# A second product half in float32r: three passes for the even blocks, two banks a block, and a ring of token columns

## The chip, the cores and the metric

The kernel runs on one core of a Trainium2 chip. The time is device microseconds of that core, from start to end of one execution. Five engines take part, each with a queue of its own that it works through in order: PE (matrix products; its weight loads are shown as PEld), ACT, DVE and POOL (operations on tiles, element by element), and SP, which here only issues DMA transfers. SBUF is the memory on the chip, with 128 partitions; PSUM is the memory that PE writes its products to, in eight banks of 128 x 512 float32. An engine waits for another through semaphores.

## What is computed

Two stages. The first is an attention with a polynomial feature map, for 4 batches x 4 heads x 1088 tokens of 32 numbers:

```
phi(x)[i, j] = (S1 @ x)[i] * (S2 @ x)[j]          # 8 x 8 = 64 features
kv = sum over tokens of phi(k) v;  z = sum over tokens of phi(k)
attn = (phi(q) @ kv) / (phi(q) @ z + 1e-6)
```

Its result, with the four heads side by side, is x: 4352 tokens of 128 numbers. The second stage is a mixture of four experts, weighted by p, the normalised domain_probs:

```
out = sum over e of  p[:, e] * (relu(x @ w1[e]) @ w2[e])      # w1[e]: 128 x 1024, w2[e]: 1024 x 128
```

All inputs and the output are float32.

## The kernel before

**Chunks, steps and products.** The 4352 tokens are columns: x is held transposed in one SBUF tile `xT`, 128 x 4352. They are cut into eleven chunks (line 69) of 128, 448, six of 512, 320, 256 and 128 columns. A chunk takes 16 steps: 4 experts x 4 steps, and each step makes two blocks (j = 0, 1) of 128 hidden units. The first and the last chunk are "plain": PE multiplies in float32. In the nine chunks between, 144 steps in all, the first product (lines 829 to 841) goes in three passes of the faster format float32r: the weights are split into `wa`, `wb`, `wd` (`weight_parts`, line 675) and the token columns into `xa`, `xb`, `xd` (`token_parts`, line 687), so that wa·xa + wb·xb into one bank `g1` (lines 833 and 834), scaled, less wd·xd in a second bank `g2` (line 835), gives the float32 product. ACT copies `g1` to SBUF with the scale (L837), DVE subtracts `g2` (L839), and ACT applies the rectifier (L848), which is put behind the next block's copy.

**Second product.** `second` (line 850) runs two steps behind `first` (`LA = 2`). For each block PE multiplies the hidden block with `w2_sb` in float32 (L885), which the profile shows as two matmuls a block. All eight blocks of one expert, four steps, add up in one bank `o`. Then `gather` (line 909) copies the bank to `ev` on ACT (L913), multiplies it with the expert's gate on POOL (L917 or L919) and adds it to `total` (L920). After the fourth expert `turn_back` transposes `total` (L897) and stores it. In the main loop (lines 952 to 995) `gather` is only appended to the chain `ending`; its copy is issued one step later, after that step's `first` and `second`.

**PSUM.** The eight banks: two for `h` (g1), two for `g` (g2), one for `o`, one for `f` and two, `den` and `num`, for the attention.

**Order.** Nothing reorders instructions: the order in which the program issues them is each engine's queue. The attention is written as a generator of small pieces (`front`, line 760; a unit of query columns has 20 pieces, a batch's keys 19), and `work()`, called after each block of a step, issues as many pieces as the remaining attention needs to be done in time (`rate`, line 959; a reserve of eight pieces). About half of the pieces hold a DVE operation, a few a group of PE matmuls through the helper of line 204. Results of the attention go to a DRAM tile `xd` and back into `xT` through SP's queue (lines 611 to 623). `token_parts` for the next chunk is issued in the last step of a chunk (line 972), gates are loaded at the steps of line 982, and `weight_parts` is issued one piece a step from step 7 on (line 970).

Of the kernel before, what the change touches and what calls it, by code (L numbers as in the profile page):

```python
# [24 lines left out]
def kernel(  # L25
# [52 lines left out]
    ps_h = ctx.enter_context(tc.tile_pool(name="ps_h", bufs=2, space=bass.MemoryType.PSUM))  # L78
    ps_g = ctx.enter_context(tc.tile_pool(name="ps_g", bufs=2, space=bass.MemoryType.PSUM))
# [48 lines left out]
    w1_sb = cpool.tile([P, E, F], F32, name="w1_sb")  # L128
    w2_sb = cpool.tile([P, E, FB, DM], F32, name="w2_sb")

    def load_w1(e):
        nc.sync.dma_start(w1_sb[:, e, :], w1[e])

    def load_w2(e):
        nc.sync.dma_start(w2_sb[:, e], w2[e].rearrange("(f p) d -> p f d", p=P))
# [25 lines left out]
    load_w2(0)  # L161
    for e in range(1, E):
        load_w1(e)
        load_w2(e)
    sk = cpool.tile([P, P], F32, name="sk")
    sp = cpool.tile([32, 3, 2, 32], F32, name="sp")
# [147 lines left out]
    def load_gates(m, experts):  # L314
        for e in experts:
            gate[m, e] = mpool.tile([P, CW], F32, tag="gate", bufs=6, name="gate")
            for b, c, n, at in parts(m):
                nc.sync.dma_start(gate[m, e][:, at : at + n], gates[b, e, c : c + n].partition_broadcast(P))

    xT = cpool.tile([P, B * S], F32, name="xT")  # L320
# [46 lines left out]
    def key_project_wide(b, gi, kf):  # L367

        t0, n = FG[gi]
        if gi == 0:  # L370
            fss[b] = apool.tile([P, 2, NT, 32], F32, tag="fs", name="fs")
            kps[b] = apool.tile([P, NT, 2, P], F32, tag="kp", name="kp")
        for t in range(n):
            for _ in range(2):
                on_side(
                    lambda s: kf[half[s], P * t : P * t + P],
                    lambda s: kT[:, P * (t0 + t) + HP * s : P * (t0 + t) + HP * s + HP],
                    lambda s: sk[:, :],
                    start=True,
                    stop=True,  # L380
                )
        nc.scalar.copy(
            _ap(fss[b], 0, P, 32 * t0, [[32 * NT, 2], [32, n], [1, 32]]), _ap(kf, 0, P, 0, [[32, 2], [P, n], [1, 32]])
        )
# [126 lines left out]
    def attend_first(b, c, n, qp):  # L511

        nd = [psum(ps_n, "den"), psum(ps_n, "num")]
        for _ in range(2):
            on_side(
                lambda s: nd[0][half[s], 0:n],
                lambda s: _ap(vx, 0, P, D, [[0, HP]]),
                lambda s: _ap(eps, 0, P, 0, [[0, n]]),
                start=True,
                stop=False,  # L520
            )
        for i in range(2):
            for _ in range(2):
                on_side(
                    lambda s: nd[i][half[s], 0:n],
                    lambda s: kvzs[b][:, s, 1 - i, :],
                    lambda s: qp[s][:, 0:n],
                    start=(i > 0),
                    stop=True,
                )  # L530
        yield

        rc = apool.tile([P, 2, HP], F32, tag="rd", name="rd")
        for i in range(2):
            by_g = [[32, 4], [1, 16]]
            nc.vector.reciprocal(_ap(rc, 0, P, HP * i, [[16, 4], [1, 16]]), _ap(nd[0], 0, P, 16 * i, by_g))
            nc.vector.tensor_tensor(
                out=_ap(xT, 0, P, HP * i, [[1, 4], [4, 16]]),
                in0=_ap(nd[1], 0, P, 16 * i, by_g),
                in1=_ap(rc, 0, P, HP * i, [[16, 4], [1, 16]]),  # L540
                op=ALU.mult,
            )
        have[0] += n
        yield

    def attend(b, c, n, qp):
# [46 lines left out]
        for c0, T, t0 in laid:  # L593
# [4 lines left out]
            if b == 0 and c == P:  # L598
                for x in range(2):
                    yield  # L600
                    for a in (x, x + 2):
                        run = 32 * T[a // 2]
                        for h in range(H):
                            copy = nc.scalar.copy if h % 2 else nc.gpsimd.tensor_copy
                            at = S * b + c + a // 2 * 64 * T[0] + a % 2 * run
                            copy(xT[32 * h : 32 * h + 32, at : at + run], _ap(y, 32 * a, 32, 32 * T[0] * h, [[1, run]]))
                continue
            m = 64 * sum(T)
            base = xd.offset + P * (S * b + c + c0)
            for a in range(4):  # L610
# [9 lines left out]
            nc.sync.dma_start(  # L620
                xT[:, S * b + c + c0 : S * b + c + c0 + m],
                bass.AP(xd.tensor, base, [[m, P], [1, m]]),
            )
# [5 lines left out]
    def queries(b, c, n):  # L629
        qc = early.pop((b, c), None)  # L630
        if qc is None:
            qT = query_turn(b, c, n)
            yield
            yield
            yield
            qc = psum(ps_f, "f")
            both(qc[:, 0:n], sq[:, :], qT[:, 0:n], start=True, stop=True)
            yield
# [28 lines left out]
    NEAR = 1.0 - 2.0 ** -13  # L667
    wa = cpool.tile([P, E, F], F32R, name="wa")
# [6 lines left out]
    def weight_parts(e):  # L675

        HF = F // 2
        for c in (slice(0, HF), slice(HF, F)):
            nc.scalar.activation(wa[:, e, c], w1_sb[:, e, c], ACTF.Copy, scale=4096.0 * NEAR)
            stt(wb[:, e, c], w1_sb[:, e, c], 4096.0, wa[:, e, c].bitcast(F32), ALU.subtract)  # L680
            yield
            stt(wd[:, e, c], wa[:, e, c].bitcast(F32), R12, wb[:, e, c].bitcast(F32), ALU.subtract)
            yield

    xparts = {}

    def token_parts(m):
# [3 lines left out]
        x = xT[:, START[m] : START[m] + n]  # L691
        nc.scalar.activation(xa[:, 0:n], x, ACTF.Copy, scale=R12 * NEAR)  # L692
        stt(xb[:, 0:n], xa[:, 0:n].bitcast(F32), -4096.0, x, ALU.add)
        nc.vector.tensor_tensor(  # L694
# [4 lines left out]
    def start():  # L699
# [9 lines left out]
        for gi in range(3):  # L709
            kf.append(psum(ps_h, "h") if gi < 2 else psum(ps_g, "g"))  # L710
# [7 lines left out]
        fq = [psum(ps_o, "o"), psum(ps_g, "g"), psum(ps_n, "num")]  # L718
# [34 lines left out]
        early[b, n] = psum(ps_g, "g")  # L753
# [28 lines left out]
    def half_columns(i, hp, c):  # L782

        e, f = divmod(i, NP)
        for j in range(2):
            both(
                hp[:, P * j + c : P * j + c + HP],
                w1_sb[:, e, P * (2 * f + j) : P * (2 * f + j + 1)],
                xT[:, c : c + HP],
                start=True,  # L790
                stop=True,
            )

    def first(i, work):

        m, kq = steps[i]
        n, (e, f) = CHUNKS[m], divmod(kq, NP)
        hd = mpool.tile([P, 2 * CW], F32, tag="hid", bufs=3, name="hid")  # L800
        hid[i] = hd

        if plain(m):
            rectify()
# [5 lines left out]
            else:  # L810
                hp = psum(ps_h, "h")
                for j in range(2):
                    both(
                        hp[:, n * j : n * j + n],
                        w1_sb[:, e, P * (2 * f + j) : P * (2 * f + j + 1)],
                        xT[:, START[m] : START[m] + n],
# [12 lines left out]
        xa, xb, xd_ = (x[:, 0:n] for x in xparts[m])  # L829
        for j in range(2):  # L830
            c = slice(P * (2 * f + j), P * (2 * f + j + 1))
            g1, g2 = psum(ps_h, "h"), psum(ps_g, "g")
# [3 lines left out]
            out = hd[:, n * j : n * j + n]  # L836
            nc.scalar.activation(out, g1[:, 0:n], ACTF.Copy, scale=1.0 + R12)  # L837
            rectify()
            nc.vector.tensor_tensor(out=out, in0=out, in1=g2[:, 0:n], op=ALU.subtract)  # L839
            to_rectify.append(out)  # L840
            work()

    to_rectify = []

    def rectify():
        while to_rectify:
            out = to_rectify.pop(0)
            nc.scalar.activation(out, out, ACTF.Relu)  # L848

    def second(i):  # L850
# [3 lines left out]
        if plain(m):  # L854

            if f == 0:
                acc[m] = psum(ps_g, "g") if e % 2 else psum(ps_o, "o")
            for j in range(2):
                for _ in range(2):
                    on_side(  # L860
                        lambda s: acc[m][half[s], 0:DM],
                        lambda s: hd[:, n * j + HP * s : n * j + HP * s + HP],
                        lambda s: w2_sb[:, e, 2 * f + j, :],
# [3 lines left out]
            if f == NP - 1:  # L867
                p_e = ends[:, 1 if m else 0, e : e + 1]
                if e == 0:
                    total[m] = mpool.tile([P, P], F32, tag="end", name="end")  # L870
# [11 lines left out]
        if f == 0:  # L882
            acc[m, e] = psum(ps_o, "o")
        for j in range(2):
            nc.tensor.matmul(  # L885
                acc[m, e][:, 0:n],
                w2_sb[:, e, 2 * f + j, :],
                hd[:, n * j : n * j + n],
                start=(f == j == 0),
                stop=(f == NP - 1 and j == 1),  # L890
            )
# [17 lines left out]
    def gather(m, e):  # L909
# [3 lines left out]
        nc.scalar.copy(ev[:, 0:n], acc.pop((m, e))[:, 0:n])  # L913
        g = gate.pop((m, e))[:, 0:n]
        if e == 0:
            total[m] = mpool.tile([P, CW], F32, tag="total", name="total")
# [4 lines left out]
        yield  # L921
        if e == E - 1:
# [24 lines left out]
    for i in range(3):  # L947
        begun_hp[i] = psum(ps_h, "h") if i < 2 else psum(ps_g, "g")
        half_columns(i, begun_hp[i], 0)
    to_part = chain.from_iterable(weight_parts(e) for e in range(E))  # L950
    ending = iter(())
    for i in range(len(steps) + LA):
        if i < len(steps):
# [5 lines left out]
            rate = CHUNKS[m] / NQ * max([0] + [(needed[c] + (8 if c > 1 else 4) - done[0]) / (START[c] - gone) for c in range(m + 1, NC)])  # L959
# [10 lines left out]
            if i > NQ - 10:  # L970
                next(to_part, None)
            if kq == NQ - 1 and m + 2 < NC:
# [9 lines left out]
            if m and m + 2 < NC and kq in (LA + 3, NQ - 4):  # L982
                load_gates(m + 1, range(2) if kq == LA + 3 else range(2, E))
# [5 lines left out]
        if i >= LA:  # L989
            second(i - LA)  # L990
            mm, kk = steps[i - LA]
            if kk % NP == NP - 1 and not plain(mm):
                ending = chain(ending, gather(mm, kk // NP))
# [31 lines left out]
```

## Time and profile before

| | us |
|---|---|
| median of three runs (581.96 to 583.17) | 582.67 |
| the profiled execution | 583.37 |
| its span, first to last instruction | 581.6 |
| first plain chunk, attention's start and weights | 0 to 31.4 |
| nine chunks in float32r, 144 steps | 31.4 to 559.1 |
| rest, last plain chunk | 559.1 to 581.6 |
| PE busy in the span | 507.9 |
| ACT, DVE, POOL busy | 328.0, 308.6, 85.4 |

A group in the profile is a line of the kernel, its engine and operation, the tiles it writes and reads, how often it ran, its busy time, the mean duration of one, and the idle time of the engine before it with what ended it. The list of waits sums such idle times: who waited for whom, total, times, longest. A timeline row is start, duration, engine, line, operation, tiles and form; the bracket holds the idle time before it. A matmul's row begins when PE may start it and its end is modelled; the distance between the starts of neighbouring rows tells how long PE was held by one.

### The profile page before, as it was taken

To read this page: it belongs to the slowest core of one execution; us is meant where nothing else is said; L and a number is where in the kernel's file an instruction comes from. 1 tells how busy PE (TensorE), PEld (TensorE's weight loads), DVE (VectorE), ACT (ScalarE), POOL (GpSimd) and SP (SyncE) were. 2 spreads that over 40 slices of the span, in tenths; PEclk is the share of its full clock that TensorE was granted. 3 is DMA by queue.
4 is the path that set the end of the run, shared out by engine and by line. 5 is a ranking of instruction groups with operands and counts; after the bars stand their busy time and mean duration, and the time that the engine had idled before them with its cause. 6 is when DMAs were issued, how large, how long until landed. Compare 5 with 4: busy or idle time off the path is not lost.

```text
span 581.6 us, 8014 instructions
## 1 busy us (share of the span) xinstructions
PE 507.9 (87%) x2823; PEld 320.4 (55%) x2823; DVE 308.6 (53%) x649; ACT 328.0 (56%) x693; POOL 85.4 (15%) x109
## 2 busy tenths in 40 slices
PE   9888888988888979989798898888989988897887
PEld 6855555554454544655454454545445554676777
DVE  6978544564745445375655355246473454444433
ACT  3665565555564664565556565355565565565651
POOL 5200110111110101101110101101101011212110
PEclk9998999999998999999999898889999999999999
DMA  8672140002002042010204011010200200020000
GB/s 226 192 157 64 40 150 19 20 16 73 0 12 67 0 116 72 19 19 17 52 0 92 1 46 18 19 17 2 61 15 11 53 11 10 15 60 0 13 1 16
DMA packets 42576, 26.04 MB, mean 45 GB/s; under 512 B 25928, under 2 KB 38568, under 8 KB 42536
## 3 DMA queue, kind: packets, MB, share of 16 engines
q1 hardware_dynamic: 42520, 25.53, 17.4%
q8 instruction: 22, 0.36, 0.3%
q14 instruction: 18, 0.15, 0.1%
q10 hardware_dynamic: 16, 0.00, 0.0%
HBM read 21.28 MB, written 4.24 MB: 44 GB/s over the span
## 4 chain that ended last, share of the span: by engine, by line
PE 73%; ACT 15%; DVE 8%; issue 2%; DMA 1%; POOL 0%; ACTq 0%; SPq 0%; DVEq 0%
PE o L885 39%; PE h L833 9%; PE h L834 9%; PE g L835 8%; ACT hid L837 6%; ACT hid L848 5%; PE f L204 3%; ACT ev L913 3%; PE den L204 2%; PE h L204 2%; DVE hid L839 1%; DVE qp L504 1%; DVE xd L694 1%; DVE xb L673 1%; PE g L204 1%
## 5 line engine op out<-in xcount | busy, mean ns | idle before, releaser
L839 DVE TENSOR_TENSOR hid<-hid,g 128x512 f32<-128x512 f32 (+3 forms) x288 | 180.3, 626 | 248.1 <-PE h L834 121.4
L885 PE MATMUL o<-hid,w_sb 128*128 128x512 f32 (+3 forms) x576 | 258.0, 572 | 56.3 <-ACT ev L913 56.3
L837 ACT ACTIVATE hid<-h 128x512 f32<-128x512 f32 (+3 forms) x288 | 157.5, 547 | 219.6 <-PE h L834 218.1
L885 PEld LDWEIGHTS o<-hid,w_sb 128*128 128x128 f32 x576 | 105.9, 193 | 136.2 <-ACT ev L913 68.9
L848 ACT ACTIVATE hid<-hid 128x512 f32<-128x512 f32 (+3 forms) x288 | 166.5, 578 | 1.2 <-DVE hid L839 1.2
L833 PE MATMUL h<-xa,wa 128*128 128x512 f32 (+3 forms) x288 | 160.5, 557 | 2.8 <-ACT xa L692 2.4
L834 PE MATMUL h<-xb,wb 128*128 128x512 f32 (+3 forms) x288 | 107.7, 374 | 4.8 <-DVE xb L673 4.7
L835 PE MATMUL g<-xd,wd 128*128 128x512 f32 (+3 forms) x288 | 108.3, 376 | 2.9 <-DVE xd L694 1.6
L919 POOL TENSOR_TENSOR ev<-ev,gate 128x512 f32<-128x512 f32 (+3 forms) x27 | 31.5, 1165 | 342.4 <-ACT ev L913 342.4
L833 PEld LDWEIGHTS h<-xa,wa 128*128 128x128 f32 x288 | 55.7, 193 | 44.5 <-issue 22.4
L834 PEld LDWEIGHTS h<-xb,wb 128*128 128x128 f32 x288 | 55.3, 192 | 38.8 <-issue 26.1
L835 PEld LDWEIGHTS g<-xd,wd 128*128 128x128 f32 x288 | 54.5, 189 | 15.6 <-DVE xd L694 4.3
L920 POOL TENSOR_TENSOR total<-total,ev 128x512 f32<-128x512 f32 (+3 forms) x27 | 31.4, 1164 | 2.1
L917 POOL TENSOR_TENSOR total<-ev,gate 128x512 f32<-128x512 f32 (+3 forms) x9 | 10.8, 1196 | 119.4 <-ACT ev L913 107.0
L504 DVE TENSOR_TENSOR qp<-qa,qb 64x512 f32<-64x512 f32 (+5 forms) x44 | 25.3, 574 | 1.0
L204 PE MATMUL h<-xT,w_sb 128*64 128x128 f32 (+1 forms) x256 | 18.5, 268 | 1.9 <-ACT hid L825 1.9
L825 ACT ACTIVATE hid<-h 128x256 f32<-128x256 f32 x22 | 8.2, 383 | 20.7 <-PE h L204 20.6
L913 ACT COPY ev<-o 128x512 f32<-128x512 f32 (+3 forms) x36 | 19.2, 534 | 0.0
L204 PEld LDWEIGHTS h<-xT,w_sb 128*64 128x64 f32 x256 | 14.1, 137 | 3.8 <-ACT hid L825 2.1
L650 DVE STREAM_SHUFFLE qa<-qf 128x512 f32<-128x512 f32 (+5 forms) x22 | 12.9, 586 | 0.0
L394 DVE TENSOR_TENSOR kp<-fs 128x256 f32<-128x256 f32 (+1 forms) x24 | 10.8, 452 | 0.1
L204 PEld LDWEIGHTS den<-kvx,qp 128*64 128x64 f32 x240 | 8.4, 137 | 3.6 <-PE h L834 2.1
(142 smaller groups left out, 251.2 us busy)
## 6 DMA issues: line engine op xcount, KB each, us to landing
w_sb<-in_moe_w_dram SPq DMA_DIRECT2D x8, 512.0 KB
gate<-gates SPq DMA_DIRECT2D x16, 256.0 KB
kn<-in_k_dram SPq DMA_DIRECT2D x4, 544.0 KB
vn<-in_v_dram SPq DMA_DIRECT2D x16, 128.0 KB
gate<-gates SPq DMA_DIRECT2D x8, 224.0 KB
qn<-in_q_dram SPq DMA_DIRECT2D x2, 544.0 KB
out_dram<-ob SPq DMA_DIRECT2D x16, 64.0 KB
qn<-in_q_dram SPq DMA_DIRECT2D x2, 480.0 KB
```

What stands on the lines that cost most here:

```text
L204: nc.tensor.matmul(out(s), weights(s), moving(s), **flags)
L504: nc.vector.tensor_tensor(out=qp[p][64 * x : 64 * x + 64, 0:n], in0=qa[64 * p : 64 * p + 64, 0:n], in1=qb[64 * p : 64 * p + 64, 0:n], op=A ...
L833: nc.tensor.matmul(g1[:, 0:n], wa[:, e, c], xa, start=True, stop=False)
L834: nc.tensor.matmul(g1[:, 0:n], wb[:, e, c], xb, start=False, stop=True)
L835: nc.tensor.matmul(g2[:, 0:n], wd[:, e, c], xd_, start=True, stop=True)
L837: nc.scalar.activation(out, g1[:, 0:n], ACTF.Copy, scale=1.0 + R12)
L839: nc.vector.tensor_tensor(out=out, in0=out, in1=g2[:, 0:n], op=ALU.subtract)
L848: nc.scalar.activation(out, out, ACTF.Relu)
L885: nc.tensor.matmul(acc[m, e][:, 0:n], w2_sb[:, e, 2 * f + j, :], hd[:, n * j : n * j + n], start=(f == j == 0), stop=(f == NP - 1 and j == 1),
L913: nc.scalar.copy(ev[:, 0:n], acc.pop((m, e))[:, 0:n])
L919: nc.gpsimd.tensor_tensor(out=ev[:, 0:n], in0=ev[:, 0:n], in1=g, op=ALU.mult)
L920: nc.gpsimd.tensor_tensor(out=total[m][:, 0:n], in0=total[m][:, 0:n], in1=ev[:, 0:n], op=ALU.add)
```

## The change

The second product of the even block (j = 0) of each step also goes in three float32r passes. `FK = 1` says that it is the even ones alone.

- The weights: `second_weight_parts` makes `va`, `vb`, `vd` from the even half of w2[e] (one ACT and two DVE operations an expert). They take the memory of w1[e] and w2[e]'s even half, so `load_last` fetches those again for the last chunk, in the middle of the chunk before it.
- The hidden block: instead of one rectifier, ACT makes `hb` and `ha` (`high_parts`), DVE forms `hb` from t and `hb` (`low_parts`, both operands in SBUF) and POOL subtracts them to `hc`. The odd block keeps its rectifier. A tile `t` with two buffers stands between; its buffer is free when both have read it.
- Banks: the expert's sum needs two, `o0` and `o1`. `h` now has three banks for g1 and g2 together; `g` is gone.
- `gather` copies both banks on ACT (`ev`, `ew`) and adds them on POOL ahead of the gate. Its first part is issued at once, in the step that ends the block. The gate of the same expert for the next chunk is loaded one step later; the gates have four buffers in place of six.
- `token_parts` is issued three steps earlier (step 12 of 16, but for the first chunk), and its last operation moves from DVE to POOL. The pace of the pieces aims four steps earlier.
- `xT` is replaced by a ring of three chunks and two small tiles for the plain chunks.
- The weight pieces start two steps earlier. `key_project_wide` and a query product issue one full matmul where two half-column calls stood.

```
     def token_parts(m):
...
-        x = xT[:, START[m] : START[m] + n]
+        ((x, _, _),) = placed(START[m], n)
...
-        nc.vector.tensor_tensor(
+        nc.gpsimd.tensor_tensor(
             out=xd_[:, 0:n], in0=xa[:, 0:n].bitcast(F32), in1=xb[:, 0:n].bitcast(F32), op=ALU.subtract
         )
...
         for j in range(2):
             c = slice(P * (2 * f + j), P * (2 * f + j + 1))
-            g1, g2 = psum(ps_h, "h"), psum(ps_g, "g")
+            g1, g2 = psum(ps_h, "h"), psum(ps_h, "h")
...
-            out = hd[:, n * j : n * j + n]
-            nc.scalar.activation(out, g1[:, 0:n], ACTF.Copy, scale=1.0 + R12)
-            rectify()
-            nc.vector.tensor_tensor(out=out, in0=out, in1=g2[:, 0:n], op=ALU.subtract)
-            to_rectify.append(out)
+            t = mpool.tile([P, CW], F32, tag="t", name="t")[:, 0:n]
+            nc.scalar.activation(t, g1[:, 0:n], ACTF.Copy, scale=1.0 + R12)
+            flush(ACT)
+            nc.vector.tensor_tensor(out=t, in0=t, in1=g2[:, 0:n], op=ALU.subtract)
+            flush()
+            if j < FK:
+                ha, hb, hc = (mpool.tile([P, CW], F32R, tag=f"h{i}", bufs=3, name=f"h{i}")[:, 0:n] for i in "abd")
+                hid[i].append((ha, hb, hc))
+                later[ACT].append(lambda t=t, ha=ha, hb=hb: high_parts(t, ha, hb))
+                later[DVE].append(lambda t=t, ha=ha, hb=hb, hc=hc: low_parts(t, ha, hb, hc))
+            else:
+                u = hidden()[:, 0:n]
+                hid[i].append(u)
+                later[ACT].append(lambda t=t, u=u: nc.scalar.activation(u, t, ACTF.Relu))
             work()
...
+    def high_parts(t, ha, hb):
+        nc.scalar.activation(hb, t, ACTF.Relu, scale=NEAR)
+        nc.scalar.activation(ha, t, ACTF.Relu, scale=NEAR * R12)
+
+    def low_parts(t, ha, hb, hc):
+        nc.vector.scalar_tensor_tensor(
+            out=hb, in0=t, scalar=0.0, in1=hb.bitcast(F32), op0=ALU.max, op1=ALU.subtract
+        )
+        nc.gpsimd.tensor_tensor(out=hc, in0=ha.bitcast(F32), in1=hb.bitcast(F32), op=ALU.subtract)
...
-            acc[m, e] = psum(ps_o, "o")
+            acc[m, e] = psum(ps_o, "o0"), psum(ps_o, "o1")
+        o0, o1 = (o[:, 0:n] for o in acc[m, e])
+        last = f == NP - 1
         for j in range(2):
...
+            if j < FK:
+                (va, vb, vd), (ha, hb, hc) = w2_parts[e], hd[j]
+                nc.tensor.matmul(o0, va[:, f, :], ha, start=(f == j == 0), stop=False)
+                nc.tensor.matmul(o0, vb[:, f, :], hb, start=False, stop=(last and j == FK - 1))
+                nc.tensor.matmul(o1, vd[:, f, :], hc, start=(f == j == 0), stop=False)
+            else:
+                nc.tensor.matmul(o1, w2_of[e, j][:, f, :], hd[j], start=False, stop=(last and j == 1))
...
     def gather(m, e):
...
-        nc.scalar.copy(ev[:, 0:n], acc.pop((m, e))[:, 0:n])
+        ew = mpool.tile([P, CW], F32, tag="ew", bufs=1, name="ew")
+        o0, o1 = acc.pop((m, e))
+        nc.scalar.activation(ev[:, 0:n], o0[:, 0:n], ACTF.Copy, scale=1.0 + R12)
+        nc.scalar.copy(ew[:, 0:n], o1[:, 0:n])
+        nc.gpsimd.tensor_tensor(out=ev[:, 0:n], in0=ev[:, 0:n], in1=ew[:, 0:n], op=ALU.add)
...
         yield
+        if not plain(m + 1):
+            load_gates(m + 1, [e])
...
-            if i > NQ - 10:
+            if i > NQ - 12:
                 next(to_part, None)
-            if kq == NQ - 1 and m + 2 < NC:
+            if kq == NQ - (4 if m else 1) and m + 2 < NC:
...
+            if m == NC - 2 and kq == NQ // 2:
+                while have[0] < B * S:
+                    piece()
+                load_last()
...
             if kk % NP == NP - 1 and not plain(mm):
-                ending = chain(ending, gather(mm, kk // NP))
+                ended = gather(mm, kk // NP)
+                next(ended)
+                ending = chain(ending, ended)
```

## The prediction

> **What bounds the kernel now.** I read the table of engines first, then PE's waits, then the timeline of two ordinary steps and one that opens an expert's block, then the starts of all 144 steps. The profiled execution took 583.37 us for a span of 581.6 us; the sum below is made against 583.37, which is 0.7 us above the median of the runs, 582.67.
>
> ```profile
> PE 507.9 (87%) x2823; PEld 320.4 (55%) x2823; DVE 308.6 (53%) x649; ACT 328.0 (56%) x693; POOL 85.4 (15%) x109
> ...
> L885 PE MATMUL o<-hid,w_sb 128*128 128x512 f32 (+3 forms) x576 | 258.0, 572 | 56.3 <-ACT ev L913 56.3
> ```
> ```profile
> PE o L885 <- ACT ev L913: 56.3, 35, 3.0
> PE h L834 <- DVE xb L673: 4.7, 8, 0.8
> PE h L833 <- ACT xa L692: 2.4, 5, 1.4
> ```
> PE is the bound; no other engine is busy 60% of the span. What PE waits for is almost only the copy of the finished block out of its single bank. The timeline shows the two kinds of step (start, duration, engine, line):
>
> ```profile
> 145.90 0.19 PEld L833 LDWEIGHTS h<-xa,wa 128*128 128x128 f32 x1 [0.24 <-issue]
> ...
> 146.33 0.19 PEld L834 LDWEIGHTS h<-xb,wb 128*128 128x128 f32 x1 [0.24 <-issue]
> ...
> 146.56 0.39 PE L834 MATMUL h<-xb,wb 128*128 128x512 f32 x1
> ...
> 147.05 0.60 ACT L837 ACTIVATE hid<-h 128x512 f32<-128x512 f32 x1 [0.99 <-PE h L834]
> ...
> 147.55 0.62 ACT L848 ACTIVATE hid<-hid 128x512 f32<-128x512 f32 x1
> 147.68 0.69 DVE L839 TENSOR_TENSOR hid<-hid,g 128x512 f32<-128x512 f32 x1 [0.97 <-PE h L834]
> ...
> 149.06 0.59 ACT L913 COPY ev<-o 128x512 f32<-128x512 f32 x1
> ...
> 149.70 0.30 PEld L885 LDWEIGHTS o<-hid,w_sb 128*128 128x128 f32 x2 [2.26 <-ACT ev L913]
> ...
> 151.09 0.19 PEld L833 LDWEIGHTS h<-xa,wa 128*128 128x128 f32 x1 [0.24 <-issue]
> ```
> Steps begin with a weight load of L833. An ordinary step of 512 columns is 3.11 us: its float32r matmuls start 0.23 us apart (six, 1.38), and each of the four halves of the two float32 ones takes 0.43 (1.72). The step above runs from 145.90 to 151.09, 5.19 us, because ACT reaches the copy at 149.06, behind both halves of the next step. So a block's end costs 2.08 us. Over all steps the ordinary ones are 2.72, 3.11, 1.96 and 1.575 us for 448, 512, 320 and 256 columns: 16 x (2.72 + 6 x 3.11 + 1.96 + 1.575) = 398.6 us of the 527.7 us between 31.4 and 559.1. The 36 ends of blocks add 24 x 2.08 + 4 x 1.93 + 4 x 1.62 + 4 x 1.5 = 70 us, chunk starts (waits for xa, xb, xd) about 15, half-clock stretches about 12 (granted clock 0.979 of 581.6 us), attention's matmuls the rest. PE explains the whole middle.
>
> **The terms.** Call a step's first-product matmuls a0 b0 d0 and a1 b1 d1.
>
> 1. *Passes.* One float32 block (2 x 0.43) becomes three float32r (3 x 0.23): -0.17 us a step at 512, and by the same two lengths -0.14, -0.08, -0.04 at 448, 320, 256. 96 x 0.17 + 16 x 0.26 = **-20.5**.
>
> 2. *Three banks where there were four.* Four tiles a step now rotate through three banks, so d1 takes the bank that a0 and b0 filled and waits until ACT has copied it. In the step above b0 streams from 146.56 to 146.79 and the copy starts at 147.05, so 0.72 us after a0's stream begins (146.33); it takes 0.595; PE goes on 0.05 later (ev's end at 149.65, the load at 149.70) and a restart costs 0.11 more (a restarted first half is 0.53 long, not 0.43). d1 ends its stream at 0.72 + 0.595 + 0.05 + 0.11 + 0.23 = 1.705 where it ended at 1.38: +0.325 us. For 448, 320, 256 columns, with their copies of 0.541, 0.434, 0.381: +0.35, +0.40, +0.43. 96 x 0.325 + 16 x 1.18 = +50; some 22 of attention's groups of matmuls (half of some 45) lie between d0 and a1 and cover it: -7. **+43**. So a 512 step goes to 3.11 - 0.17 + 0.325 = 3.26 us: the passes alone lose.
>
> 3. *Block ends.* The copies go into ACT's queue before the next step, onto banks that the next block needs 1.7 us later: -70. What comes instead: two copies (0.5 us apart) hold back the next step's first copy by 0.24 us, and with it d1. Then POOL runs hc, add, multiply, add back to back (4 x 1.28). DVE's new operation (it forms hb from two SBUF operands) can't run beside a POOL operation:
>
> ```profile
> 149.73 1.27 POOL L919 TENSOR_TENSOR ev<-ev,gate 128x512 f32<-128x512 f32 x1 [12.76 <-ACT ev L913]
> 149.95 1.39 DVE L504 TENSOR_TENSOR qp<-qa,qb 64x320 f32<-64x320 f32 x1
> ```
> That L504 form takes 0.48 to 0.49 us in the rows around it; here it ends 0.34 after POOL does. In the other order POOL is stretched (L917 at 118.56: 1.69 us). Laid out by queue, the next step's hb operation is ready about 0.2 us after the multiply has begun and starts 1.07 later; 0.3 of that is slack, 0.75 reaches the following step's first copy, whose buffer t it must free. A chance phase costs less. Between 0.24 and 1.0 us a block; I take 0.9 at 512, in proportion below: **-70 + 29**.
>
> 4. *Tokens.* Chunk starts lose their 15 us; xa, xb (two SBUF operands) and xd, now on POOL at 1.28, cost the steps they fall into about 0.9 each: **-7**. The new tokens need their DMAs four steps earlier; the pace aims at that point with eight pieces to spare, some 3.5 steps, so I cost it at nothing. A late DMA would stop ACT, and PE behind it. SP's gate loads now wait for POOL's multiply, about one step, inside the same reserve.
>
> 5. *DVE and ACT.* ACT gets five operations a step at 0.5 us apart (147.05, 147.55), 2.5, and 0.25 for copies: below 3.26, so no bound. DVE gets three at 0.61 to 0.69 beside attention's 0.8 a step (128 us busy from 200 to 450; the two L839 of the 61 steps in there are 82, so 46 over 61 steps): 2.8 of 3.26. The loop from one step's first copy through subtract, a piece of attention w, subtract and hb to the next first copy is 2.57 + w us, free up to w = 0.69. Single pieces (0.4 to 0.73) fit; a double, about one in six calls, costs up to 0.6, and a product or hb caught by POOL about 0.4. No row shows the queues this full: between 0 and +45; I take **+18**, near the low end, as most pieces fit by their rows.
>
> 6. *Second weights* (4 x one ACT and two DVE operations, 0.63 and 0.69) in the stretch to 60 us, where DVE is busy 16 of every 20 us: 0 to +12, **+7**. The reload of 3.1 MB for the last chunk begins some 15 us before it; at the 169 GB/s of the first 55 us all of it takes 18.6, and the last expert is wanted some 10 us into the chunk. **+1**.
>
> 7. *Clock.* Each half-clock stretch follows a long stop of PE, and most of those stops go: of the 12 us about 3 stay, **-9**. The profile shows no stretch after short stops. The Trainium skill ("TensorE: Matmul & The Clock Gate", section "A second HAM failure mode: psum-queue depth-cycling") speaks against this change: it tells of a kernel whose short idles, from cycling through banks, made the clock fall and recover again and again. That is what term 2 makes; if each of 36 blocks met one stretch of 3.4 us at half speed, my estimate from it would be about +49 us in place of -9. No row here shows it.
>
> Removed half-column calls for keys and queries (0.27 us matmuls two at a time) against full ones: nothing either way, between -2 and +2.
>
> **Sum:** -20.5 + 43 - 41 - 7 + 18 + 7 + 1 - 9 = -8.5: 575 us in the profiled execution, **574** beside the median.
>
> **Rivals.**
> *A, the new waits are mostly covered.* Attention's matmuls and a drifting phase hide them: block ends cost 0.24 (8 us, not 29), term 5 costs 6 and term 2 33. All of it gives 574 - 21 - 12 - 10 = 531, half of it 552: I put **541**. For it: PE was the only full engine. Against: d1's wait is built into every step.
>
> *B, slower: the SBUF read that DVE and POOL share becomes the cycle.* POOL goes from 85 to about 300 us busy (hc 96 x 1.28, 16 x 1.13, 0.87, 0.73, and a third operation a block). If hb or a product waits half a POOL operation (0.64) in every step that carries a piece of attention (w = 0.55), the loop is 2.57 + 0.55 + 0.64 = 3.76, not 3.26: +0.5 in some 75 steps, 38 us, of which 12 are in term 5: **600**. It decides from w + wait above 0.69 us; whether hc falls beside attention's products is set by phase, and I can't exclude it.
>
> *C, a long wait stays.* hc comes late at block ends, or the two copies wait on each other, and half the 70 us remain: 574 + 35 - 15 (the collisions that then fall into the wait) = **594**.
>
> *D, it doesn't do what it says:* the three passes aren't faster than two halves. The six rows of 0.23 speak against that; 574 + 20 = **594**.
>
> **Chances.** Forecast (560 to 581) 0.40; A 0.20; B 0.28; C 0.08; D 0.04. Forecast and A make 0.60 faster and the others 0.40 slower; of these 0.04 and 0.01 lie within 0.2% of 582.67, about what a measurement of this kernel can tell from no change: faster 0.56, same 0.05, slower 0.39. Range: most of A and most of B, **545 to 606**.
>
> **What would show it.** Right: PE's wait on the block's copy gone from its list, a wait of d1 on the first ACT copy in nearly every step (some 0.2 us), ordinary 512 steps of 3.2 to 3.3 us, hb operations longer than 0.69 only beside POOL. Wrong: ordinary steps near 2.94 (term 2), 3.7 and more (B), or half-clock stretches well above seven (term 7).

## The result, and the profile after

The changed kernel takes 575.71 us (median of four runs, 574.72 to 576.13), the kernel before beside it 582.32: a ratio of 0.988, 95% interval 0.986 to 0.990. The prediction said 574. The profiled execution's span went from 581.6 to 572.9 us. Read by stage, from the starts of the 144 steps in both timelines:

| us | before | after | difference |
|---|---|---|---|
| up to the first float32r step | 31.4 | 32.7 | +1.3 |
| chunk of 448 columns | 58.4 | 70.9 | +12.5 |
| six chunks of 512 | 396.2 | 372.8 | -23.4 |
| chunk of 320 | 42.4 | 42.1 | -0.3 |
| chunk of 256 and the rest | 53.2 | 54.4 | +1.2 |

So the six chunks of 512 became 6% faster, and the 448 chunk, which makes the new weights, gave half of that back. The page's table of engines and the top groups of the changed kernel:

```profile
PE 501.9 (88%) x2893; PEld 337.0 (59%) x2893; DVE 432.4 (75%) x792; ACT 424.5 (74%) x877; POOL 318.6 (56%) x298
...
L901 POOL TENSOR_TENSOR hd<-ha,hb 128x512 fp32r<-128x512 f32 (+3 forms) x144 | 173.2, 1203 | 206.5 <-PE h L872 74.9
...
L875 ACT ACTIVATE t<-h 128x512 f32<-128x512 f32 (+3 forms) x288 | 158.9, 552 | 100.9 <-DVE hb L898 47.3
...
L898 DVE SCALAR_TENSOR_TENSOR hb<-t,hb 128x512 fp32r<-128x512 f32 (+3 forms) x144 | 113.8, 790 | 0.3 <-ACT hb L894 0.3
```

and what PE waits for in it (total, times, longest):

```profile
PE h L873 <- ACT t L875: 45.3, 83, 1.6
PE h L871 <- DVE t L877: 11.2, 15, 1.6
PE o L952 <- DVE vd L685: 2.5, 1, 2.5
```

PE is busy for hardly less time than before, three other engines have filled up, and the wait on the block's copy (56.3 us) is gone from the list. In its place stands d1 (second call of L873), which waits for the step's first copy (L875). The timeline of an ordinary step shows it:

```profile
303.60 0.19 PEld L871 LDWEIGHTS h<-xa,wa 128*128 128x128 f32 x1 [0.24 <-issue]
...
303.87 0.68 DVE L898 SCALAR_TENSOR_TENSOR hb<-t,hb 128x512 fp32r<-128x512 f32 x1
...
304.74 0.60 ACT L875 ACTIVATE t<-h 128x512 f32<-128x512 f32 x1 [0.47 <-PE h L872]
...
305.39 0.19 PEld L873 LDWEIGHTS h<-xd,wd 128*128 128x128 f32 x1 [0.48 <-ACT t L875]
...
306.86 0.19 PEld L871 LDWEIGHTS h<-xa,wa 128*128 128x128 f32 x1 [0.24 <-issue]
```

303.60 to 306.86 is 3.26 us; the copy ends at 305.34 and d1's load starts at 305.39. And this is the second step after a block's end, 4.16 us long:

```profile
299.44 0.19 PEld L871 LDWEIGHTS h<-xa,wa 128*128 128x128 f32 x1 [0.24 <-issue]
...
299.54 1.28 POOL L986 TENSOR_TENSOR ev<-ev,gate 128x512 f32<-128x512 f32 x1
299.72 1.66 DVE L898 SCALAR_TENSOR_TENSOR hb<-t,hb 128x512 fp32r<-128x512 f32 x1
...
301.49 0.60 ACT L875 ACTIVATE t<-h 128x512 f32<-128x512 f32 x1 [1.38 <-DVE hb L898]
...
302.14 0.19 PEld L873 LDWEIGHTS h<-xd,wd 128*128 128x128 f32 x1 [1.38 <-ACT t L875]
```

hb is issued 0.18 us after the gate's multiply has begun on POOL, stands until that ends, frees t at 301.38, and only then can the first copy write t and d1 go on. 35 of the 144 hb operations are stretched by over 0.15 us, by 24 us together. Each of the 35 overlaps a POOL operation: 32 began beside the additions and the multiply of a block's end, 3 beside hc. The Trainium skill ("SBUF — State Buffer", section "Who interferes with whom") says that a DVE operation with two SBUF inputs contends with a POOL operation that reads SBUF, that the shared ports are an exclusive lock, and that the order of issue decides which of the two is blocked. The trace agrees: hb takes 1.66 us in place of 0.68 and ends 0.56 us after the multiply does.

### The profile page after: what moved, and what is told of

Its sections match the earlier page's. It is cut to its first block, busy times and chain, and to the rows that moved or that the text cites. A ratio compares the mean times of both kernels' runs of the same rounds, so it can differ in the third digit from the quotient of the medians.

```text
span 572.9 us, 9123 instructions
## 1 busy us (share of the span) xinstructions
PE 501.9 (88%) x2893; PEld 337.0 (59%) x2893; DVE 432.4 (75%) x792; ACT 424.5 (74%) x877; POOL 318.6 (56%) x298
## 4 chain that ended last, share of the span: by engine, by line
PE 40%; DVE 27%; ACT 23%; issue 7%; DMA 1%; ACTq 0%; POOL 0%; SPq 0%; DVEq 0%
ACT t L875 13%; DVE t L877 9%; PE o L954 9%; DVE hb L898 9%; PE h L873 8%; PE h L871 4%; PE h L872 4%; ACT hid L887 3%; PE o L950 3%; PE o L951 3%; DVE qp L517 3%; PE o L952 3%; ACT hb L894 3%; ACT ha L895 2%; PE h L208 2%
## 5 line engine op out<-in xcount | busy, mean ns | idle before, releaser
L901 POOL TENSOR_TENSOR hd<-ha,hb 128x512 fp32r<-128x512 f32 (+3 forms) x144 | 173.2, 1203 | 206.5 <-PE h L872 74.9
L877 DVE TENSOR_TENSOR t<-t,h 128x512 f32<-128x512 f32 (+3 forms) x288 | 179.8, 625 | 116.6 <-ACT t L875 89.5
L875 ACT ACTIVATE t<-h 128x512 f32<-128x512 f32 (+3 forms) x288 | 158.9, 552 | 100.9 <-DVE hb L898 47.3
L871 PE MATMUL h<-xa,wa 128*128 128x512 f32 (+3 forms) x288 | 162.7, 565 | 12.6 <-DVE t L877 11.2
L873 PE MATMUL h<-xd,wd 128*128 128x512 f32 (+3 forms) x288 | 121.2, 421 | 48.6 <-ACT t L875 45.3
L954 PE MATMUL o<-hid,w_sb 128*128 128x512 f32 (+3 forms) x288 | 135.7, 553 | 0.0
L873 PEld LDWEIGHTS h<-xd,wd 128*128 128x128 f32 x288 | 54.4, 189 | 103.8 <-ACT t L875 96.9
L898 DVE SCALAR_TENSOR_TENSOR hb<-t,hb 128x512 fp32r<-128x512 f32 (+3 forms) x144 | 113.8, 790 | 0.3 <-ACT hb L894 0.3
L894 ACT ACTIVATE hb<-t 128x512 fp32r<-128x512 f32 (+3 forms) x144 | 83.0, 576 | 16.0 <-DVE t L877 14.3
L871 PEld LDWEIGHTS h<-xa,wa 128*128 128x128 f32 x288 | 55.1, 191 | 58.4 <-DVE t L877 26.6
L887 ACT ACTIVATE hid<-t 128x512 f32<-128x512 f32 (+3 forms) x144 | 83.4, 579 | 0.0
L895 ACT ACTIVATE ha<-t 128x512 fp32r<-128x512 f32 (+3 forms) x144 | 82.5, 573 | 0.0
L952 PE MATMUL o<-hd,vd 128*128 128x512 f32 (+3 forms) x144 | 54.1, 376 | 3.1 <-DVE vd L685 2.5
L950 PE MATMUL o<-ha,vab 128*128 128x512 f32 (+3 forms) x144 | 55.0, 382 | 0.0
L952 PEld LDWEIGHTS o<-hd,vd 128*128 128x128 f32 x144 | 27.4, 190 | 8.4 <-POOL ev L986 2.8
```

The lines of the kernel that those rows point to most:

```text
L871: nc.tensor.matmul(g1[:, 0:n], wa[:, e, c], xa, start=True, stop=False)
L873: nc.tensor.matmul(g2[:, 0:n], wd[:, e, c], xd_, start=True, stop=True)
L875: nc.scalar.activation(t, g1[:, 0:n], ACTF.Copy, scale=1.0 + R12)
L877: nc.vector.tensor_tensor(out=t, in0=t, in1=g2[:, 0:n], op=ALU.subtract)
L887: later[ACT].append(lambda t=t, u=u: nc.scalar.activation(u, t, ACTF.Relu))
L894: nc.scalar.activation(hb, t, ACTF.Relu, scale=NEAR)
```

## The experiments

Each was timed beside the kernel before on its own chip; its median and its ratio to that kernel are given. The first three edit the kernel before or the changed one on the question of order.

**Old kernel, copies ahead** (`old_copies_ahead`), one edit of the kernel before:

```
-                ending = chain(ending, gather(mm, kk // NP))
+                ended = gather(mm, kk // NP)
+                next(ended)
+                ending = chain(ending, ended)
```

> The kernel before with one edit: the block's copy is issued in the step that ends the block, as in the changed kernel; one bank for the block, no three-pass second product. My theory: the 2.08 us that a block's end cost before was order on ACT's queue alone. PE wants the bank 1.38 us after the block's last matmul, the copy starts about 0.26 after it and takes 0.58, so the wait is gone and some 0.3 us a block stays: 70 - 11 = 59 us, and some 7 us of half-clock stretches go with the stops: 582 becomes about 515 (505 to 525). Rival: the copy needs the second bank, because ACT runs behind PE and reaches the copy late in spite of its place: about 1 us a block stays, 545.

Measured: 509.79 us, ratio 0.873 (0.871 to 0.875). PE's waits no longer hold the block's copy at all:

```profile
PE h L834 <- DVE xb L673: 4.8, 8, 0.8
PE h L833 <- ACT xa L692: 2.4, 5, 1.4
PE h L204 <- ACT hid L825: 1.9, 1, 1.9
```

Steps that open a block are 3.11 like the others, and the granted clock rose from 0.979 to 0.997. The wait was order alone; no second bank was needed, and this edit is worth eleven times the whole change. Some 10 of its 74 us are the clock's: half-clock stretches lose half their length, 11.9 us in the span of the kernel before and 1.7 here.

**The same with early tokens** (`old_copies_tokens`): also the changed kernel's condition for `token_parts` (line 1047) and its pace (`left`), but xd on DVE.

> The same with the token pieces at step 12 of 16 and the pace of the pieces aimed four steps earlier; xd stays on DVE. My theory: chunk starts lose 15 us, and the three token operations cost about 0.5 us a chunk where they fall: 10 us below the kernel with the copies ahead alone, about 505. Rival: they cost in the middle of the chunk what they cost at its start, or a late DMA stops ACT: within 3 us of it, or slower.

Measured: 495.16 us, ratio 0.848 (0.847 to 0.850); 14.6 us less, nearly all of the 15 that chunk starts cost (1.7 of it is the clock's: no half-clock stretch is left).

**New kernel, copies late** (`new_copies_late`): the first edit taken out of the changed kernel.

> The changed kernel with the block's copies issued one step later, as in the kernel before. My theory: the block's end costs 2.08 us and 0.5 for the second copy again, in place of the 1.3 us that it costs now: 36 x 1.2 = 43 us more, about 618 (605 to 630). Rival: DVE and POOL are the limit after a block's end anyway, and catch up while PE waits: 590.

Measured: 658.57 us, ratio 1.128 (1.125 to 1.130). Neither number holds.

```profile
PE o L950 <- ACT ev L978: 66.3, 35, 3.2
```

The mean granted clock is 0.925: 49 us of the span lost to half clock, where the changed kernel loses 7. Without these losses the span is 41 us longer than the changed kernel's (606.9 against 566.1), where the theory had 43. So its mechanism fits; the clock was left out of it.

So order alone is worth 88 us in the old kernel, and the changed kernel holds that order. The three passes with all that the change brings for them (banks, t, hc, the ring, the reload, xd on POOL) must then cost some 80 us. The next experiments look for these in the changed kernel.

**Four buffers for t** (`new_four_t2`):

```
-            t = mpool.tile([P, CW], F32, tag="t", name="t")[:, 0:n]
+            t = mpool.tile([P, CW], F32, tag="t", bufs=4, name="t")[:, 0:n]
...
-                ha, hb, hc = (mpool.tile([P, CW], F32R, tag=f"h{i}", bufs=3, name=f"h{i}")[:, 0:n] for i in "abd")
+                ha, hb, hc = (mpool.tile([P, CW], F32R, tag=f"h{i}", bufs=3 if i == "b" else 2, name=f"h{i}")[:, 0:n] for i in "abd")
```

Four buffers for t and three for ha and hc don't fit: the pool would take 60.5 kB a partition of the 57.2 that are left. So ha and hc have two here.

> The changed kernel with four buffers for t, and two in place of three for ha and hc, which makes the room. My theory: a held hb operation reaches PE only through t's buffer (47 us of ACT's waits, most of them in the second step after a block's end, 4.16 us against 3.26). It should come to about 548 (540 to 556). Rival: DVE's own queue is the limit, since the subtract behind a held hb is late too: 570.

Measured: 551.57 us, ratio 0.945 (0.938 to 0.951): 24 us. The second step after a block's end is 3.27 in 12 of the 24 blocks of 512 columns; in the changed kernel one is that short. hb is held at least as much as before (28 us in 42 operations), but it no longer holds back the first copy, and d1's wait for that copy falls from 45.3 us to:

```profile
PE h L873 <- ACT t L875: 12.6, 36, 1.3
PE h L871 <- DVE t L877: 14.9, 17, 1.6
```

**No hc on POOL** (`new_no_hc`): `low_parts` without its second line, `hc = hb`.

> The changed kernel without POOL's subtraction hc; the third pass reads hb in its place, so part of the computation is left out. DVE's and ACT's work is as it was. My theory: what POOL costs is the read that it shares with DVE (24 us by which 35 hb operations are held): gone but for the block ends' own POOL operations, about 545 (535 to 555), near the kernel with four buffers for t. Rival: POOL's part is small and the first copies are late because of ACT's and DVE's own queues: 568.

Measured: 555.18 us, ratio 0.952 (0.946 to 0.959), 20 us (3 of it the clock's).

```profile
ACT t L875 <- DVE hb L899: 38.4, 51, 2.3
```

ACT still waits for hb: 29 hb operations are stretched, by 12 us together, each beside one of the block ends' POOL operations. So hc is part of the hold-up, not all of it.

**A fourth bank** (`new_four_banks`): `ps_h` with four buffers, one tag for `o`, all four matmuls of the second product into it.

```
-            acc[m, e] = psum(ps_o, "o0"), psum(ps_o, "o1")
+            acc[m, e] = [psum(ps_o, "o0")] * 2
```

> The changed kernel with a fourth bank for the first product, taken from the block's sum: all four matmuls of the second product add into one bank, so the scale of part of the sum is wrong; both copies and POOL's addition stay, so ACT's and POOL's work is as it was. My theory: the wait of d1 on the first copy goes from every step: an ordinary 512 step of 2.94 us, and 30 to 43 us less, 540 (532 to 548), if DVE's loop through t does not take over in steps that carry attention. Rival: it takes over in most of them: ordinary steps 2.94 but 560 in all.

Measured: 569.62 us, ratio 0.977 (0.971 to 0.982): 6 us only, less than both. Ordinary steps are 2.95 as both said, but ACT waits 46 us for hb, and PE's wait for the first copy has turned into one for the subtract:

```profile
ACT t L875 <- DVE hb L898: 45.8, 60, 2.1
PE h L873 <- DVE t L877: 22.6, 29, 1.4
PE o L950 <- ACT ew L979: 8.4, 18, 1.0
```

The edit also brings costs of its own: the wait for the second copy (8.4 us), a first float32r step at 40.0 us, 7 later, and half-clock stretches that lose 15 us in place of 7.

**Both** (`new_four_t_banks`).

> The kernel with the fourth bank (all of the block's sum in one bank, so the scale of part of it is wrong) and four buffers for t, two for ha and hc. The fourth bank alone gave 6 us, and ACT waited 46 us for hb operations there. My theory now: d1's wait and hb's hold-up lie beside each other, so that taking one away uncovers the other, and the bank is worth its price once t is free: from the 552 of four buffers for t, 30 us less in the steps, and 15 more for this kernel's single bank (8 us of PE's wait for the second copy, 7 in the first plain chunk): about 537. Rival: DVE is the floor of the steps with attention, bank or no bank: 555 or more.

Measured: 537.36 us, ratio 0.920 (0.915 to 0.926). The bank is worth 14 us once t is free, and some 15 more that this kernel's single `o` costs by the expectation's estimate (the first float32r step starts at 39.8 us, 7 later). The number came as expected, but that the two waits lie beside each other isn't shown. In the six 512 chunks, without what half-clock stretches lose there, the changed kernel takes 371.1 us, with the bank alone 355.6, with t's buffers alone 353.8 and with both 338.5: some 15 and 17 us singly, 33 together. There the two add up. What left the bank alone at 6 us is the price of the single `o`, which both kernels pay, and 9 us more of lost clock.

**Both, and no hc** (`new_banks_t_no_hc`).

> The kernel with four banks and four buffers for t, and without POOL's subtraction hc as well (the third pass reads hb; the scale of part of the block's sum is wrong). What is left of the three passes is PE's gain and ACT's and DVE's extra operations, with POOL's at block ends. My theory: with t free, what POOL holds up no longer reaches PE except through DVE's queue in steps with attention and at block ends: 5 to 12 us below the 537 of the kernel with hc, about 528, and still well above the 490 of the old kernel with its edits, since ACT's and DVE's own extra work stays. Rival: POOL is what is left, and the passes come out with their gain: 510 or less.

Measured: 513.24 us, ratio 0.876 (0.870 to 0.880): 24 us less (4 of it the clock's), close to the rival's 510. My theory falls here: with t free hc still cost that much. Of these, 15 lie in the 512 chunks (341.9 to 327.0), 4 in the 448 one. PE's listed waits of L871, L873 and L952 on DVE and POOL fall from 25 to 14, beside 3.5 for vd in both:

```profile
PE h L873 <- DVE t L877: 14.4, 21, 1.4
PE h L871 <- DVE t L877: 6.4, 9, 1.0
PE o L952 <- POOL hd L901: 4.1, 7, 1.2
```
```profile
PE h L873 <- DVE t L877: 13.0, 19, 1.8
PE h L871 <- DVE t L877: 0.9, 3, 0.4
```

With hc gone the third pass no longer waits for POOL either (the 4.1 us), so this isn't the shared read alone; which queue carries the rest I haven't settled.

**Passes between the blocks** (`new_passes_between`): four buffers for t as above, and on PE the three passes of the step two back stand between the matmuls of block 0 and block 1.

```
             work()
+            if j == 0:
+                between()          # second(i - LA, (0,)); the odd block follows after first(i)
```

> The changed kernel with four buffers for t (two for ha and hc) and with another order on PE: the three passes of the second product stand between the two blocks of the first, so that d1 comes 0.69 us later and finds the first copy done; weight pieces start one step earlier. Nothing is left out. My theory: both costs go, ordinary steps 2.94 and about 515 (505 to 528), since DVE is nearly full in steps with attention. Rival: DVE and POOL are the floor: 540.

Measured: 545.52 us, ratio 0.934 (0.929 to 0.940). Ordinary steps are 2.95, but only 6 us less than with four buffers for t (half-clock stretches lose 3 more): passes that come earlier meet the block's copy.

```profile
PE o L952 <- ACT ev L980: 18.0, 25, 1.2
PE h L871 <- DVE t L877: 6.9, 9, 1.3
```

**The same but for a block's first step** (`new_between_but_first`).

> The kernel with the passes between the blocks, but in the first step of an expert's block they stand behind both blocks again, since PE waited 18 us there for the copy of the block before (25 times). My theory: those 18 us go and 36 steps pay 0.33 again, 12 us: 546 becomes about 539. Rival: the wait only moves to the same ACT queue's first copy: 545.

Measured: 548.01 us, ratio 0.939 (0.933 to 0.944). The copy's 18 us are gone; d1's wait on the first copy and a0's on the subtract have taken their place:

```profile
PE h L871 <- DVE t L877: 18.8, 19, 1.6
PE h L873 <- ACT t L875: 16.6, 28, 1.3
```

So there is no gain. The rival was nearer, though only part of the wait moved to the first copy.

**Fewer second-weight operations** (`new_less_second_weights`): `second_weight_parts` without its two DVE lines.

> The changed kernel without vb and vd: the second weights' two DVE operations an expert are left out, and va stands in all three passes, so part of the computation is left out. ACT's part stays. My theory: the first chunk in float32r, 70.9 us now and 58.4 before, is long because its DVE queue holds these eight operations, of which POOL holds some up to twice their length, and PE waits 2.5 us for one of them: 62 us for the chunk and about 567 in all. Rival: it is hb and attention's catching up, and the eight operations count little: 573.

Measured: 568.71 us, ratio 0.974 (0.969 to 0.979): 7 us less, all in the 448 chunk (70.9 to 63.6). About half of it is the clock's: half-clock stretches lose 5.1 us in that chunk of the changed kernel and 1.7 here. Whether the two operations brought these stretches isn't shown. The rest of that chunk's 12.5 is not theirs.

**Full matmuls in the old kernel** (`old_full_matmuls`): `old_copies_tokens` with the change's two edits in `key_project_wide` and `queries`.

> The kernel before with copies ahead and early tokens (495 us), with the change's full matmuls for keys and queries in place of the half-column calls. I costed this edit at nothing, between -2 and +2: 493 to 497. Rival: two halves side by side keep PE shorter than one full matmul, or longer, by 0.2 us and more at some 45 places: 5 us and more either way.

Measured: 489.86 us, ratio 0.838 (0.834 to 0.843), 5.3 us less: the rival. The timeline of PE at the same place shows why, first with half-column calls, then with a full one:

```profile
203.75 0.39 PE L835 MATMUL g<-xd,wd 128*128 128x512 f32 x1
204.07 0.97 PE L204 MATMUL f<-qT,sq 128*64 128x448 f32 x4
...
205.31 0.39 PE L834 MATMUL h<-xb,wb 128*128 128x512 f32 x1
```
```profile
201.27 0.40 PE L830 MATMUL g<-xd,wd 128*128 128x512 f32 x1
201.51 0.91 PE L632 MATMUL f<-qT,sq 128*128 128x448 f32 x2
...
202.49 0.39 PE L829 MATMUL h<-xb,wb 128*128 128x512 f32 x1
```

From d0 to b1 1.56 us against 1.22. At twelve such groups, of 128 to 512 columns, the difference is 0.32 to 0.36 us whatever the width, so it isn't the half columns' own length: going over to them and back costs 0.34 us a group. This kernel is the fastest of the study, 86 us below the changed one, with no pass of the second product in float32r.

## Why the prediction was right

The total was right to 2 us, and each mechanism that it named is in the trace; some of its terms were off, in both directions, so that it came this close is luck in part.

1. *Passes*, -20.5, and 2. *three banks*, +43: right to the step. 3.26, 2.30 and 2.01 us were measured for 512, 320 and 256 columns; the terms give 3.26, 2.28 and 1.96. At 448 hardly a step is undisturbed (2.93 by the terms). Without d1's wait (`new_four_t_banks`) the passes show: 2.95, 2.59, 1.86, 1.49. What a fourth bank gives back is less than 43: 6 us alone and 14 with t free, or some 15 in the 512 chunks once the clock is taken off.
3. *Block ends*, -70 + 29: of the -70 the old kernel's one edit shows 63 (74 us with 10 of the clock's). What comes instead was named right (two copies in ACT's queue, then hb behind the multiply, through t) and sized low: 0.38 and 0.90 us in the two steps after the first block's end in the 512 chunk that starts at 289.3, 1.28 where I took 0.9.
4. *Tokens*, -7: the -15 shows in the old kernel (14.6). In the new one they fall into steps that also follow a block's end (5.2 and 4.0 us in the chunk from 103.6); their share there isn't separated.
5. *DVE and ACT*, +18 (0 to +45): t's buffers give back 24 us, hc another 24 after t and bank. Part of both is term 3's, so the size of this term alone isn't shown. The row that I called nearest, single pieces that fit, held for steps without POOL beside them.
6. *Second weights*, +7: the edit gives 7.0, of which 3.4 in that chunk are the clock's. The wait for vd, 2.5 us, is DVE's vd held by POOL for 0.6 us at 79.39. The chunk lost 12.5 in all; what is left belongs to terms 2, 3 and 5 in a chunk where DVE also splits the first weights, and isn't separated.
7. *Clock*, -9: -5 (7 us lost now, 12 before). There are four half-clock stretches in the span, seven before. But that each follows a long stop of PE was wrong here: the four come after stops of 1.2 to 1.3 us with shorter ones behind them, and the longest stop of the middle, 2.5 us at 78.3, has none behind it. What the Trainium skill tells of short idles, a clock that falls and recovers again and again ("TensorE: Matmul & The Clock Gate", section "A second HAM failure mode: psum-queue depth-cycling"), is seen at most in these four: by the two rows shown PE stopped 98 times for a bank, up to 1.6 us each (L873 and L871). The copies-late kernel, with stops up to 3.2 us, lost 49 us.
8. *Full matmuls*, costed at nothing (-2 to +2): -5 in the old kernel.

So term 3 came out some 19 us higher (7 of the -70; by those rows 0.38 us a block at 512 and less below, 12 in all), term 7 4 higher, term 8 5 lower. Terms 2, 4 and 5 together then came out lower by about as much, and the runs don't part them. Rival B's mechanism (the read that DVE and POOL share) is in the trace, but at the block ends, not in every step: PE stays at 3.26 in steps without attention, as w + wait stays below its point there, and only 3 of the 35 stretched hb operations began beside hc.

## What to carry to other kernels

Before a product is made cheaper, look at what the bound engine waits for: here one line in the order of ACT's queue was worth 74 us, and the passes, worth 20 on PE alone, cost some 80 with all that they need. Some 62 of the changed kernel's time went with a fourth bank, two more buffers for t and POOL's hc (575.7 to 513.2, in a kernel that leaves part of the computation out); what keeps that kernel 23 us above the old one with its order and full matmuls (489.9) isn't separated. When a tile's buffer is freed by the last engine in a chain of four operations, try more buffers than the chain seems to need: two more for t gave 24 us. And before two waits are said to hide each other, compare them by stage and with the lost clock taken off: the fourth bank looked like 6 us and was some 15 in the 512 chunks, with t's buffers or without.

## What the runs showed of the hardware

A group of half-column matmuls between full ones held PE for 0.34 us longer than the same work in full matmuls (1.56 against 1.22 us above; 0.32 to 0.36 at twelve groups, at 128 columns as at 512). A half-clock stretch was 3.4 us, and in the copies-late kernel six of 23 were twice that. The length of the stop before it doesn't tell whether one comes: in the kernel before, six of the 21 stops of PE over 1.5 us had one behind them, in the changed kernel none of three, and its four followed stops of 1.2 to 1.3 us.
